# Two activation rows loaded once and spread by the array, and the first weight group moved to another DMA queue

## The chip, the cores and the metric

The kernel runs on one core of a Trainium2 chip. The metric is device time in microseconds; executions of a program can fall into a fast and a slower state, and all runs below were in the fast one, except e4, a single look without a state. Every ratio is to runs of the kernel before on the same chip. A ratio is the mean time of one kernel's runs over that of the other's of the same rounds, so it is not quite the ratio of the medians that are quoted.

## The reference, cut to what matters

One token goes through a layer norm, an attention with 32 heads over a cache of 8192 keys and values, and a gated MLP; the kernel returns the output and all gradients, including those of the two caches.

```python
# x, grad_out: (1, 1, 640)   k_cache, v_cache: (1, 32, 8192, 128)   all bf16
# wq: (640, 4096)  wo: (4096, 640)  w1, w3: (640, 1728)  w2: (1728, 640)
def _fwd_reference(...):
    xn = _layernorm(x, axis=-1)
    return x + _A_ref(xn, k_cache, v_cache, wq, wo) + _B_ref(xn, w1, w3, w2)

def reference(...):
    out, vjp = jax.vjp(f, x, k_cache, v_cache, wq, wo, w1, w3, w2)
    return (out, *vjp(grad_out))
```

Each head reads 2 MB of K and 2 MB of V and writes 2 MB of dK and 2 MB of dV. That is most of the 304 MB that the kernel moves.

## The kernel before

The SP queue is a first-in, first-out list of K and V loads, dK and dV stores and the MLP's weights. The weights wq and wo come in eight groups of four heads. Group 0 stands on the SP queue just behind K of head 0; all later groups are on the GpSimd queue. x and grad_out are loaded as broadcasts, one copy per partition, on the ACT queue.

```python
nc.scalar.dma_start(x_bc_bf, A_x.rearrange("a b d -> (a b d)").partition_broadcast(P))
nc.scalar.dma_start(g_bc[:], grad_out.rearrange("a b d -> (a b d)").partition_broadcast(P))

def load_group(g, eng):
    wq_g = wpool.tile([P, NC, GW], BF16, name="wq_g", tag="wq_g")
    eng.dma_start(wq_g[:], wq_v[:, :, g * GW:(g + 1) * GW])      # rows of 1024 B
    wo_g = wpool.tile([P, GH, D], BF16, name="wo_g", tag="wo_g")
    eng.dma_start(wo_g[:], wo_v[:, g * GH:(g + 1) * GH, :])      # rows of 1280 B
    grp[g] = dict(wq=wq_g, wo=wo_g)

lag = [1]
def load_next():                       # next K or V load, if enough of the ten slots are free
    if not pending or len(free_slots) < lag[0]:
        return
    kind, h = pending.pop(0)
    t = free_slots.pop(0)
    fifo(t[:], (kc if kind == "K" else vc)[h])        # fifo = nc.sync.dma_start
    kv_tiles[(kind, h)] = t

load_next()                            # K of head 0
load_group(0, nc.sync)
for _ in range(3):
    load_next()                        # V 0, K 1, V 1; then the MLP's weights, K 2, V 2
# ... cut ...
lag[0] = 3
```

What head 0 needs before it can multiply with the keys is prepared here. prep_q needs wq and the normalised x; prep_do needs wo and g_bc; the later steps need both.

```python
def prep_do(g, hh):
    # four dot products over wo, one per head, on VectorE
    nc.vector.scalar_tensor_tensor(junk[:], G_["wo"][:, hh, :], 1.0, g_bc[:], ALU.mult, ALU.mult,
                                   accum_out=G_["do"][:, hh:hh + 1])
# ... cut ...
T(0, "K", 0); T(0, "K", 1)
prep_q(0, ps_0[:, 0:GH], True)         # 20 small matmuls over wq
for hh in range(GH):
    prep_do(0, hh)
prep_sel(0, ...); prep_cm(0, ...); fill_qz(0); rows_pe(0, ...); rows_act(0)
for h in range(H):
    if h == MLP_AT:                    # MLP_AT = 2
        outers_a(h - 1); outers_b(h - 1)
        mlp()
    head(h)                            # stores dV and dK of head h - 1 on the SP queue, each after its outer product
```

## Time and profile before

| | before |
|---|---|
| time, median of 3 runs | 734.95 us (734.04 to 735.1) |
| bytes moved, mean rate over the span | 303.9 MB, 414 GB/s |
| wo of group 0 landed | 14.40 us |
| first maximum of head 0 | 28.55 us |
| first store issued (dV of head 0) | 44.27 us |
| dV of head 2 issued | 124.79 us |

In the profile's lines PE is the array's matmul and PEld its weight load, DVE is VectorE, ACT ScalarE, POOL GpSimd and SP SyncE; a q after the name marks an instruction of that engine's queue that issues a DMA transfer; L108 is a line of the kernel. "kv" is any of the ten slots.

Two parts of the page of the kernel before: what was moved in each of 40 equal slices, and the DMA queues with their packets, MB and share of 16 engines' span. q1 is the SP queue, q0 GpSimd's, q10 ACT's.

```profile
GB/s 337 401 410 420 425 428 423 400 421 422 417 422 426 429 427 424 427 430 426 429 425 428 429 420 427 429 429 427 425 428 427 428 432 428 428 431 429 422 390 154
...
q1 hardware_dynamic: 21328, 276.39, 89.3%
q0 software_dynamic: 5728, 26.30, 8.9%
...
q10 hardware_dynamic: 308, 0.33, 0.1%
```

The DMA is the limit. The two big queues fill 98% of the engines' time, and the rate is between 400 and 432 GB/s from the second slice to the 38th. Only the first slice and the last two are clearly lower. Time can be lost only where the queues run dry or where packets are slow.

The start, from the timeline of the kernel before (start, duration, engine, line, operation, out<-in; in brackets the idle time before it and what ended it):

```profile
1.19 0.42 SPq L108 DMA_DIRECT2D wq_g<-in_A_wq_dram  x1
1.66 0.52 SPq L110 DMA_DIRECT2D wo_g<-in_A_wo_dram  x1
...
9.96 0.10 PEld L221 LDWEIGHTS <-x_kt 1*128 1x128 bf16 x1 [9.96 <-DMA x_kt<-in_A_x_dram]
...
13.11 0.62 PEld L249 LDWEIGHTS <-wq_g 128*128 128x128 bf16 x20 [0.64 <-DMA wq_g<-in_A_wq_dram]
...
14.51 0.83 DVE L240 SCALAR_TENSOR_TENSOR side<-wo_g,g_bc 128x640 bf16<-128x640 bf16 x1 [1.05 <-DMA wo_g<-in_A_wo_dram]
...
18.75 0.17 DVE L336 COPY qz<-cm_g 128x8 bf16<-128x8 bf16 x1
```

The x broadcast lands at 9.96, wq at 13.1, and wo last: VectorE starts its dot products at 14.51, and at 18.75 the query is in place for head 0. In the pieces of the chain of waits up to 80 us there is one transfer only, this one of wo, with 12.75 us. Everything after it up to the MLP is compute. The first maxima of heads 0 and 1 come at:

```profile
28.55 0.23 DVE L355 TENSOR_REDUCE mrow<-m 128x1 f32<-128x64 f32 x1 [9.62 <-PE m L329]
47.31 0.23 DVE L355 TENSOR_REDUCE mrow<-m 128x1 f32<-128x64 f32 x1 [0.87 <-PE m L329]
```

The SP queue before its first store of head 2, from the same timeline, and the four-microsecond stretches around it (us; busy time of PE, PEld, DVE, ACT and POOL; then the array's granted clock, the busy share of the DMA engines, GB/s):

```profile
111.78 0.33 SPq L102 DMA_DIRECT2D kv<-in_A_v_cache_dram  x1
124.79 0.34 SPq L102 DMA_DIRECT2D out_dram<-kv  x1
128.07 0.33 SPq L102 DMA_DIRECT2D kv<-in_A_k_cache_dram  x1
```

```profile
120.00:124.00 4.00, 4.00 (x47) 2.36 (x44) 3.96 (x4) 2.28 (x6) 0.00 (x0) 1.00 0.97 405
124.00:128.00 4.00, 4.00 (x38) 3.07 (x35) 3.85 (x5) 2.99 (x7) 0.00 (x0) 1.00 1.01 420
128.00:132.00 4.00, 3.48 (x47) 2.60 (x46) 3.23 (x10) 2.43 (x7) 0.00 (x0) 1.00 0.99 388
```

Between 111.78 and 124.79 nothing is issued on SP. What had been issued by then lasted just long enough: the share stays at 1. So there is next to no reserve at this point (counted from the issues and the packet records, 0.2 MB of the SP queue's bytes are still under way at 124.7 us), and the store waits for compute (dV of head 2 follows its outer product on VectorE).

How the later groups fare on the GpSimd queue, from the issues of the kernel before (count, KB, median us from issue to landing):

```profile
wq_g<-in_A_wq_dram POOLq DMA_DIRECT2D x7, 640.0 KB, 13.2
wo_g<-in_A_wo_dram POOLq DMA_DIRECT2D x7, 640.0 KB, 19.5
```

### The profile page before, as it was taken

Reading aid. Unit: us, or ns where it says so; the run is one execution under the profiler, and the core shown is the slowest. Engines: PE = TensorE matmul, PEld = TensorE weight load, DVE = VectorE, ACT = ScalarE, POOL = GpSimd, SP = SyncE. Lnnn points to the kernel's source line nnn. Section 1 sums busy time; section 2 is a strip of 40 time slices with the busy share of each in tenths; the row PEclk is TensorE's granted clock in tenths of the full one; section 3 lists DMA queues with packets and bytes.
Section 4 is the critical chain, followed back from the end, with each engine's and each line's share of the span. In section 5 each row is a group of like instructions: output and inputs, shape, how many; then the busy total and the mean of one; then the engine's idle time right before and its main releaser. Section 6 shows DMA issues by size and latency. Waiting matters only on the chain.

```text
span 733.2 us, 13850 instructions
## 1 busy us (share of the span) xinstructions
PE 608.6 (83%) x5663; PEld 425.9 (58%) x5663; DVE 461.1 (63%) x806; ACT 367.9 (50%) x716; POOL 30.0 (4%) x45
## 2 busy tenths in 40 slices
PE   1998579998899889988999797888698888899840
PEld 1666457666666666665666565555475566666520
DVE  4059655677766666667767755646746576477482
ACT  1650726665465455655565554545464455554510
POOL 0010010000100000000000000000000000000000
PEclk9996699999899889988899988989989799888965
DMA  9999999999999999999999999999999999999993
GB/s 337 401 410 420 425 428 423 400 421 422 417 422 426 429 427 424 427 430 426 429 425 428 429 420 427 429 429 427 425 428 427 428 432 428 428 431 429 422 390 154
DMA packets 27428, 303.90 MB, mean 414 GB/s; under 512 B 2836, under 2 KB 4436, under 8 KB 10724
## 3 DMA queue, kind: packets, MB, share of 16 engines
q1 hardware_dynamic: 21328, 276.39, 89.3%
q0 software_dynamic: 5728, 26.30, 8.9%
q8 instruction: 44, 0.72, 0.4%
q10 hardware_dynamic: 308, 0.33, 0.1%
q14 instruction: 20, 0.16, 0.1%
HBM read 151.67 MB, written 151.34 MB: 413 GB/s over the span
## 4 chain that ended last, share of the span: by engine, by line
PE 42%; DMA 41%; ACT 7%; DVE 7%; issue 2%; SPq 0%; ACTq 0%; DVEq 0%
PE pT L294 19%; DMA kv<-in_A_k_cache_dram 18%; DMA out_dram<-kv 17%; PE m L329 6%; PE X L406 5%; ACT KT L296 4%; DMA kv<-in_A_v_cache_dram 4%; PE sA L313 3%; PE dA L313 2%; DVE kv L439 2%; DMA wo_g<-in_A_wo_dram 2%; ACT kv L589 1%; PE gu_ps L516 1%; DVE side L240 1%; ACT KT L319 1%
## 5 line engine op out<-in xcount | busy, mean ns | idle before, releaser
L296 ACT COPY KT<-pT 128x512 f32<-128x512 f32 x512 | 290.4, 590 | 235.7 <-PE pT L294 204.3
L294 PE MATMUL pT<-ident_f,kv 128*128 128x128 f32 x2048 | 321.8, 298 | 36.5 <-DMA kv<-in_A_k_cache_dram 27.3
L294 PEld LDWEIGHTS pT<-ident_f,kv 128*128 128x128 f32 x2048 | 251.7, 156 | 93.2 <-PE pT L294 29.5
L439 DVE TENSOR_TENSOR kv<-qd,U 128x4096 bf16<-128x4096 bf16 x64 | 146.1, 2285 | 0.0
L439 DVE TENSOR_TENSOR kv<-qd,P 128x4096 bf16<-128x4096 bf16 x64 | 143.6, 2285 | 0.0
L329 PEld LDWEIGHTS m<-selc,KT 128*128 128x128 f32 x512 | 67.6, 206 | 47.1 <-ACT KT L319 37.4
L329 PE MATMUL m<-selc,KT 128*128 128x16 f32 x512 | 73.7, 277 | 24.4 <-ACT KT L319 24.2
L406 PE MATMUL X<-kv,Z 128*32 128x512 bf16 x1024 | 84.9, 460 | 1.8 <-DVE Z L423 1.8
L389 DVE SCALAR_TENSOR_TENSOR U<-m,P 128x64 bf16<-128x64 f32 x32 | 7.4, 233 | 105.4 <-PE m L329 105.4
L313 PE MATMUL sA<-KT,qz 128*32 128x512 bf16 x512 | 55.4, 423 | 0.0
L313 PE MATMUL dA<-KT,qz 128*32 128x512 bf16 x512 | 54.5, 412 | 0.2 <-ACT KT L296 0.2
L313 PEld LDWEIGHTS <-qz 128*32 128x32 bf16 x1024 | 26.5, 93 | 42.7 <-issue 41.6
L406 PEld LDWEIGHTS <-Z 128*32 128x32 bf16 x1024 | 28.7, 110 | 34.0 <-issue 17.0
L355 DVE TENSOR_REDUCE mrow<-m 128x1 f32<-128x64 f32 x32 | 7.2, 224 | 60.9 <-PE m L329 60.9
L349 ACT CAST qd<-pT 128x256 bf16<-128x256 f32 x32 | 11.9, 373 | 49.3 <-DVE kv L439 31.6
L489 DVE SCALAR_TENSOR_TENSOR wq_g<-wq_g,side 128x512 bf16<-128x512 bf16 x40 | 27.3, 683 | 0.0
L240 DVE SCALAR_TENSOR_TENSOR side<-wo_g,g_bc 128x640 bf16<-128x640 bf16 x32 | 26.2, 820 | 1.4 <-DMA wo_g<-in_A_wo_dram 1.0
L362 DVE TENSOR_REDUCE negM<-m 128x1 f32<-128x128 f32 x32 | 9.3, 292 | 25.2 <-PE m L359 25.2
L421 DVE SCALAR_TENSOR_TENSOR U<-m,P 128x128 bf16<-128x128 f32 x32 | 11.4, 355 | 19.3 <-PE m L419 19.3
L379 DVE RECIPROCAL rZ<-m 128x1 f32<-128x1 f32 x32 | 5.3, 167 | 24.2 <-PE m L373 24.2
L319 ACT COPY KT<-dA 128x512 f32<-128x512 f32 x32 | 19.4, 605 | 0.6 <-PE dA L313 0.6
L319 ACT COPY KT<-sA 128x512 f32<-128x512 f32 x32 | 19.3, 602 | 0.0
(143 smaller groups left out, 363.2 us busy)
## 6 DMA issues: line engine op xcount, KB each, us to landing
out_dram<-kv SPq DMA_DIRECT2D x64, 2048.0 KB, 31.0
kv<-in_A_k_cache_dram SPq DMA_DIRECT2D x32, 2048.0 KB, 25.1
kv<-in_A_v_cache_dram SPq DMA_DIRECT2D x32, 2048.0 KB, 26.3
out_dram<-wo_g POOLq DMA_DIRECT2D x8, 640.0 KB, 12.0
out_dram<-wq_g POOLq DMA_DIRECT2D x8, 640.0 KB, 13.0
wq_g<-in_A_wq_dram POOLq DMA_DIRECT2D x7, 640.0 KB, 13.2
wo_g<-in_A_wo_dram POOLq DMA_DIRECT2D x7, 640.0 KB, 19.5
kv<-in_B_w_dram SPq DMA_DIRECT2D x2, 1728.0 KB, 27.1
```

Source lines behind the costliest of these rows:

```text
L240: nc.vector.scalar_tensor_tensor(junk[:], G_["wo"][:, hh, :], 1.0, g_bc[:], ALU.mult, ALU.mult, accum_out=G_["do"][:, hh:hh + 1])
L294: nc.tensor.transpose(pT[:, k * P:(k + 1) * P], W3[:, 4 * c + k, :], ident_f[:])
L296: nc.scalar.copy(KT[:].rearrange("p k w -> p (k w)"), pT[:])
L313: nc.tensor.matmul(S_[kind][q:q + QW, :], lhsT=S_["qz"][:, o:o + QW], rhs=KTb[:, par, :], start=(c0 == 0), stop=(c0 == NCH - 2), skip_grou ...
L319: nc.scalar.copy(XS[:].rearrange("p k w -> p (k w)"), S_.pop(kind)[:])
L329: nc.tensor.matmul(S_["m"][:, b0:b0 + J].rearrange("p (c k t) -> p k c t", k=4, t=2)[:, k, :, :], lhsT=XS[:, k, :], rhs=selc[:].rearrange( ...
L349: nc.scalar.copy(qd[:].rearrange("p a d -> p (a d)"), hd[h].pop("ps_r"))
L362: nc.vector.tensor_reduce(S_["negM"][:], S_["m"][:, 2 * J:2 * J + P], AX.X, ALU.max, negate=True)
L406: nc.tensor.matmul(xg["X"][q:q + QW, :], lhsT=Z[:, o:o + QW], rhs=W[:, N4 * i:N4 * (i + 1)], start=(slot == 0 and i < 4), stop=(slot == NS ...
L421: nc.vector.scalar_tensor_tensor(S_["U2"][:], S_["V"][:, 0:J].unsqueeze(2).to_broadcast([P, J, 2]), S_["m"][:, OC + NS:OC + NS + 1], S_["P ...
L439: nc.vector.tensor_tensor(dst[:, lo * DH:hi * DH].rearrange("p (j a b) -> p j a b", a=DH // 2, b=2), vec.rearrange("p (a b) -> p a b", b=2 ...
L489: nc.vector.scalar_tensor_tensor(wq_g[:, ci, :], wq_g[:, ci, :], 1.0, dqb, ALU.mult, ALU.mult, accum_out=dxa[:, ci, g:g + 1])
```

## The change

The intent was to drop 0.33 MB of broadcasts, to get x early, and to let the first weight group run beside K of head 0 in place of standing behind it. The diff in full:

```diff
--- before.py
+++ after.py
@@ -92,11 +92,14 @@
     NSLOT = 10
     RW = 64
 
-    x_kt = tpool.tile([P, 4, P], F32, name="x_kt", tag="KT")
-    x_bc_bf = x_kt[:].rearrange("p k w -> p (k w)").bitcast(BF16)[:, 0:D]
-    nc.scalar.dma_start(x_bc_bf, A_x.rearrange("a b d -> (a b d)").partition_broadcast(P))
+    rows_in = []
+    for src in (A_x, grad_out):
+        r_kt = tpool.tile([P, 4, P], F32, name="row_kt", tag="KT")
+        row = r_kt[0:1].rearrange("p k w -> p (k w)").bitcast(BF16)[:, 0:D]
+        nc.scalar.dma_start(row, src.rearrange("a b d -> (a b) d"))
+        rows_in.append(row)
+    x_row, g_row = rows_in
     g_bc = consts.tile([P, D], BF16, name="g_bc")
-    nc.scalar.dma_start(g_bc[:], grad_out.rearrange("a b d -> (a b d)").partition_broadcast(P))
 
     def fifo(out_, in_):
         nc.sync.dma_start(out_, in_)
@@ -125,7 +128,7 @@
         kv_tiles[(kind, h)] = t
 
     load_next()
-    load_group(0, nc.sync)
+    load_group(0, nc.gpsimd)
     for _ in range(3):
         load_next()
     mC = free_slots.pop(0)
@@ -209,22 +212,30 @@
         return ps_t.tile([P, 512], F32, name="pT", tag="pT")
 
     ln3 = consts.tile([P, 3], F32, name="ln3")
-    msum, sumsq, std = ln3[:, 0:1], ln3[:, 1:2], ln3[:, 2:3]
-    nc.vector.tensor_reduce(msum, x_bc_bf, AX.X, ALU.add)
-    nc.vector.tensor_scalar(negmean[:], msum, -1.0 / D, None, ALU.mult)
-    nc.vector.scalar_tensor_tensor(t_tile()[:, 0:D], x_bc_bf, negmean[:], x_bc_bf, ALU.add, ALU.mult,
-                                   accum_out=sumsq)
-    nc.scalar.activation(std, sumsq, ACTF.Sqrt, bias=eps_t[:], scale=1.0 / D)
-    nc.vector.reciprocal(rstd[:], std)
+    xsum, sumsq, std = ln3[:, 0:1], ln3[:, 1:2], ln3[:, 2:3]
     ps_xg = pst()
+    ps_g = pst()
     for ci in range(NC):
-        nc.tensor.matmul(ps_xg[:, ci:ci + 1], lhsT=x_bc_bf[0:1, ci * P:(ci + 1) * P], rhs=one_bf[0:1, :],
+        nc.tensor.matmul(ps_xg[:, ci:ci + 1], lhsT=x_row[:, ci * P:(ci + 1) * P], rhs=one_bf[0:1, :],
                          start=True, stop=True)
-        nc.tensor.matmul(ps_xg[:, NC + ci:NC + ci + 1], lhsT=g_bc[0:1, ci * P:(ci + 1) * P], rhs=one_bf[0:1, :],
+        nc.tensor.matmul(ps_xg[:, NC + ci:NC + ci + 1], lhsT=g_row[:, ci * P:(ci + 1) * P], rhs=one_bf[0:1, :],
                          start=True, stop=True)
+    nc.tensor.matmul(ps_xg[:, P:P + D - 512], lhsT=one_bf[0:1, :].to_broadcast([1, P]), rhs=g_row[:, 512:D],
+                     start=True, stop=True)
+    nc.tensor.matmul(ps_g[:], lhsT=one_bf[0:1, :].to_broadcast([1, P]), rhs=g_row[:, 0:512],
+                     start=True, stop=True)
+    nc.scalar.copy(g_bc[:, 0:512], ps_g[:])
+    nc.scalar.copy(g_bc[:, 512:D], ps_xg[:, P:P + D - 512])
     nc.vector.tensor_copy(x_col[:], ps_xg[:, 0:NC])
     nc.vector.tensor_copy(g_col[:], ps_xg[:, NC:2 * NC])
-    nc.vector.tensor_scalar(xn_col[:], x_col[:], negmean[:], rstd, ALU.add, ALU.mult)
+    nc.vector.tensor_reduce(xsum, x_col[:], AX.X, ALU.add)
+    nc.tensor.matmul(ps_xg[:, 16:17], lhsT=ones_b, rhs=xsum, start=True, stop=True)
+    nc.vector.tensor_scalar(negmean[:], ps_xg[:, 16:17], -1.0 / D, None, ALU.mult)
+    nc.vector.scalar_tensor_tensor(xn_col[:], x_col[:], negmean[:], x_col[:], ALU.add, ALU.mult, accum_out=sumsq)
+    nc.tensor.matmul(ps_xg[:, 17:18], lhsT=ones_b, rhs=sumsq, start=True, stop=True)
+    nc.scalar.activation(std, ps_xg[:, 17:18], ACTF.Sqrt, bias=eps_t[:], scale=1.0 / D)
+    nc.vector.reciprocal(rstd[:], std)
+    nc.vector.tensor_scalar(xn_col[:], x_col[:], negmean[:], rstd[:], ALU.add, ALU.mult)
     nc.vector.tensor_copy(xn_col_bf[:], xn_col[:])
 
     def prep_new(g):
@@ -791,7 +802,7 @@
     nc.vector.tensor_scalar(nst[:], ps_f[:, 0:2], -1.0 / D, None, ALU.mult)
     t5 = consts.tile([P, NC], F32, name="t5")
     nc.vector.scalar_tensor_tensor(t5[:], xn_col[:], nst[:, 1:2], dxn[:], ALU.mult, ALU.add)
-    nc.vector.tensor_scalar(t5[:], t5[:], nst[:, 0:1], rstd, ALU.add, ALU.mult)
+    nc.vector.tensor_scalar(t5[:], t5[:], nst[:, 0:1], rstd[:], ALU.add, ALU.mult)
     nc.vector.tensor_tensor(fin[:, NC:2 * NC], t5[:], g_col[:], ALU.add)
     ps_o = pst()
     nc.tensor.transpose(ps_o[0:2 * NC, 0:P], fin[:], ident_f[:])
```

## The prediction

> What bounds the kernel. The transfers: the table of queues gives the SP queue 89.3% and the GpSimd queue 8.9% of the 16 engines' time. 303.9 MB move at 414 GB/s mean, 428 in later slices, 337 in the first. Time is bytes over rate, plus start, tail, and any stretch in which the queues run dry.
>
> The start hangs on compute. The chain of waits up to 78 us is: transfer of the first wo group (12.75 us, lands 14.40), four dot products on VectorE (0.86 us each), head 0, head 1, the MLP; no KV load is in it. Issued minus finished bytes, the backlog is used up near 125 us, when head 2's V store is issued (124.79, after waiting for VectorE). Afterwards the backlog grows to 5 MB by 300 us: transfers set the pace and a lost microsecond is not regained. So a delay of head 0 comes through nearly in full.
>
> What the change does.
> 1. The two broadcasts (0.33 MB, rows of 1280 B) become two rows. By the packet records they held the engines about 1.2 us: saved. x lands at 3 to 4 us in place of 9.94.
> 2. Norm statistics and the spread of grad_out move to the array: some ten steps of 0.15 to 0.6 us, 3 to 4 us against 3 before, done before the weights land. Neutral.
> 3. wq and wo of group 0 leave the SP queue, where they stood just behind K of head 0, for the GpSimd queue. On SP they moved in 1024 and 1280 B packets[...]; on GpSimd packets are 4096 and 5120 B (160 to 200 ns): about 0.8 us saved. But later groups show what that queue costs beside a full SP queue: 4.2 us from issue to first packet, then one small packet for each 16 KB packet of SP. That engines take turns between queues packet by packet is also what the Trainium skill says ("DMA: Bandwidth & Descriptors", Queues, rings and completion order); the trace agrees (equal packet counts of both queues while a group loads). Issue to landing is 13.2 us for wq and 19.5 us (17.6 to 21.0) for wo, issued 0.9 us later. Issued at 0.7 us, wo lands at about 21, not 14.4.
>
> Sum: head 0 starts 5 to 7 us later; head 2's store moves to about 131; the DMA idles there, and the 2 us of transfer saved only widen the hole. Net about +5 us.
>
> Predicted: 740 us, 8 in 10 between 735 and 744.5. Faster by over 2%: 0.01; within: 0.96; slower: 0.03.
>
> Right if: wo of group 0 lands at 19 to 22 us and the first dot product starts there; the first maximum of head 0 (28.55) moves to 33 to 36; the first store (44.27) to 49 to 51; head 2's V store to 129 to 132, with DMA share clearly below 1 just before it; x lands before 5 us; GB/s from 2 to 10 us rises. Wrong if: wo lands before 15 us, head 0 has caught up by 125 us, or the DMA stays full there.
>
> What would make it wrong. The GpSimd queue may start quicker at an empty start, or get larger turns; then only the saving of 1 to 2 us is left (733). The granted clock is half from 57.7 to 71.4 and from 78 to 92 us; another phase may give or take some us of the MLP.

## More of the kernel before

The experiments ran on several chips, where the median of the kernel before was between 733.68 and 734.95 us, so two versions of different rounds are compared by their ratios.

The MLP uses four of the ten slots for its weights and gives them back when its gradients are stored.

## The result and the profile after

| | before | after |
|---|---|---|
| time, median of 6 runs each | 734.83 us | 740.35 us (738.44 to 742.38) |
| ratio, with 95% interval | | 1.0075 (1.0054 to 1.0095) |
| span of the profiled run | 733.2 us | 738.7 us |

The 0.75% is clear of noise.

The start of the kernel after, from its timeline:

```profile
1.29 0.99 POOL L111 DMA_DIRECT2D wq_g<-in_A_wq_dram  x1 [0.84 <-POOLq L828]
1.30 0.23 ACTq L99 DMA_DIRECT2D row_kt<-in_grad_out_dram  x1
2.05 0.10 PEld L219 LDWEIGHTS <-row_kt 1*128 1x128 bf16 x1 [2.05 <-DMA row_kt<-in_A_x_dram]
2.28 0.77 POOL L113 DMA_DIRECT2D wo_g<-in_A_wo_dram  x1
...
6.57 0.10 PEld L221 LDWEIGHTS <-row_kt 1*128 1x128 bf16 x1 [4.41 <-DMA row_kt<-in_grad_out_dram]
...
11.37 0.17 DVE L239 CAST xn_col_bf<-xn_col 128x5 bf16<-128x5 f32 x1
...
15.19 0.61 PEld L260 LDWEIGHTS <-wq_g 128*128 128x128 bf16 x20 [3.27 <-DMA wq_g<-in_A_wq_dram]
...
21.85 0.83 DVE L251 SCALAR_TENSOR_TENSOR side<-wo_g,g_bc 128x640 bf16<-128x640 bf16 x1 [9.85 <-DMA wo_g<-in_A_wo_dram]
...
26.10 0.17 DVE L347 COPY qz<-cm_g 128x8 bf16<-128x8 bf16 x1
```

x is there at 2.05 and the normalised x at 11.5 (line L239). wq lands at 15.2, and wo at 21.85 in place of 14.40. The dot products are the same four; qz is filled at 26.10 in place of 18.75, which is 7.35 us later. The first maxima of heads 0 and 1:

```profile
36.54 0.23 DVE L366 TENSOR_REDUCE mrow<-m 128x1 f32<-128x64 f32 x1 [10.27 <-PE m L340]
53.89 0.23 DVE L366 TENSOR_REDUCE mrow<-m 128x1 f32<-128x64 f32 x1 [0.93 <-PE m L340]
```

They are 8.0 and 6.6 us later than before. The 1.4 us between go with the granted clock (see "Why the prediction was right").

The SP queue and the stretches around dV of head 2, after:

```profile
116.91 0.33 SPq L105 DMA_DIRECT2D kv<-in_A_v_cache_dram  x1
131.12 0.34 SPq L105 DMA_DIRECT2D out_dram<-kv  x1
```

```profile
120.00:124.00 4.00, 3.95 (x44) 2.45 (x44) 1.47 (x6) 3.44 (x9) 0.00 (x0) 1.00 1.07 453
124.00:128.00 4.00, 3.93 (x45) 2.66 (x42) 2.09 (x5) 1.34 (x3) 0.00 (x0) 1.00 0.47 195
128.00:132.00 4.00, 4.00 (x38) 2.79 (x37) 4.00 (x3) 2.95 (x6) 0.00 (x0) 1.00 0.07 29
132.00:136.00 4.00, 4.00 (x36) 3.18 (x36) 3.21 (x7) 2.98 (x7) 0.00 (x0) 1.00 1.07 430
```

The store is issued 6.3 us later, and from 124 to 132 us the DMA has little to do: the two shares, 0.47 and 0.07, leave 4 * 0.53 + 4 * 0.93 = 5.8 us idle. VectorE and the array are at work (2.09 and 4.00, and 3.93 and 4.00 us of each four); they are on their way to the store that would feed the DMA.

The page of the kernel after, the same parts:

```profile
GB/s 354 402 418 387 418 432 345 344 412 424 417 410 426 430 427 420 429 431 426 424 426 429 428 428 423 425 432 426 427 427 426 429 429 429 428 429 428 428 400 163
...
q10 hardware_dynamic: 24, 0.01, 0.0%
```

Slices of about 18.5 us: the first is faster (354 against 337), the seventh and eighth are the hole (345 and 344 against 423 and 400), and later ones are alike. The fourth is lower too (387 against 420): from 64 to 72 us the rate is 336 GB/s against 421, a smaller dent where the SP queue waited for the delayed stores of head 1. The engines' busy share was still 0.97 there: from 66 to 70 us they worked almost alone on the GpSimd queue's records of 4096 and 5120 B. 8 us * 85 GB/s are 0.68 MB, or 1.6 us.

**A ledger of bytes.** Summing the packet records up to 152 us gives 61.41 MB before and 58.80 MB after. The totals are 303.95 and 303.63 MB. So 242.54 MB were left before and 244.83 after, 2.29 MB more. Both kernels move 426 to 427 GB/s from 152 to 690 us, so that is 2.29 / 0.427 = 5.4 us. The spans differ by 5.5 us. The whole loss is made before 152 us.

### The profile page after: what moved, and what is told of

It is laid out like the page before. It is cut to its first block, busy times and chain, and to the rows that moved or that the text cites. A ratio compares the mean times of both kernels' runs of the same rounds, so it can differ in the third digit from the quotient of the medians.

```text
span 738.7 us, 13870 instructions
## 1 busy us (share of the span) xinstructions
PE 606.3 (82%) x5669; PEld 424.8 (58%) x5669; DVE 459.3 (62%) x806; ACT 368.3 (50%) x719; POOL 31.5 (4%) x47
## 4 chain that ended last, share of the span: by engine, by line
PE 50%; DMA 29%; ACT 9%; DVE 8%; issue 2%; ACTq 0%; POOL 0%; DVEq 0%; SPq 0%; POOLq 0%
PE pT L305 23%; DMA kv<-in_A_k_cache_dram 15%; DMA out_dram<-kv 8%; PE m L340 7%; ACT KT L307 5%; PE X L417 5%; PE sA L324 5%; DMA kv<-in_A_v_cache_dram 4%; PE dA L324 3%; DVE kv L450 3%; DMA wo_g<-in_A_wo_dram 3%; ACT KT L330 2%; DVE side L251 1%; ACT kv L600 1%; PE gu_ps L527 1%
## 5 line engine op out<-in xcount | busy, mean ns | idle before, releaser
L417 PE MATMUL X<-kv,Z 128*32 128x512 bf16 x1024 | 82.9, 451 | 1.8 <-DVE Z L434 1.8
L417 PEld LDWEIGHTS <-Z 128*32 128x32 bf16 x1024 | 28.6, 109 | 32.9 <-issue 15.2
L251 DVE SCALAR_TENSOR_TENSOR side<-wo_g,g_bc 128x640 bf16<-128x640 bf16 x32 | 26.2, 820 | 10.2 <-DMA wo_g<-in_A_wo_dram 9.8
L432 DVE SCALAR_TENSOR_TENSOR U<-m,P 128x128 bf16<-128x128 f32 x32 | 11.4, 355 | 18.9 <-PE m L430 18.9
```

Of the source, the lines that this page charges most:

```text
L417: nc.tensor.matmul(xg["X"][q:q + QW, :], lhsT=Z[:, o:o + QW], rhs=W[:, N4 * i:N4 * (i + 1)], start=(slot == 0 and i < 4), stop=(slot == NS ...
L432: nc.vector.scalar_tensor_tensor(S_["U2"][:], S_["V"][:, 0:J].unsqueeze(2).to_broadcast([P, J, 2]), S_["m"][:, OC + NS:OC + NS + 1], S_["P ...
```

## The experiments

Theory: wo of group 0 comes late on the GpSimd queue because the engines take turns between queues, one packet each, and its packets are small beside SP's; head 0 starts late; the lateness reaches dV of head 2, where the DMA has no reserve, and becomes idle DMA time. Rivals: the rows and the norm on the array cost the time; the GpSimd queue is slow by its own descriptor work; the late start costs through compute and the idle DMA is only a mark of it.

The landings in the text below are the starts of the first dot product or of the q matmuls that waited for them; the issue times are from the timelines.

### Rows without the queue, and the queue without the rows

```diff
 # e1_rows_only, on the kernel after
-    load_group(0, nc.gpsimd)
+    load_group(0, nc.sync)
 # e2_queue_only, on the kernel before
-    load_group(0, nc.sync)
+    load_group(0, nc.gpsimd)
```

> The changed kernel with group 0 back on the SP queue (rows and column-sum statistics kept). Theory (the queue of group 0 is the whole loss): wo of group 0 lands at 12 to 13.5 us, head 2's V store is issued at 122 to 124, the DMA has no hole near 126 us, and the saved broadcasts show as 1 to 2 us: 733 us. Rival (the rows, the longer norm chain or the spreading of grad_out cost the time): 738 to 740 us.

Measured: 733.02 us, ratio to before 0.9992 (0.9978 to 1.0005). wo landed at 13.36, dV of head 2 was issued at 121.52, and no stretch of 4 us from 40 to 180 us moved less than 390 GB/s.

> The kernel before with group 0 alone moved to the GpSimd queue (broadcasts kept). Theory: wo lands at 20 to 22 us, head 2's V store at 130 to 132, a DMA hole of about 5 us before it, 740 to 742 us. Rival (rows and norm part): 734 to 735 us as before.

Measured: 741.94 us, ratio 1.0109 (1.0095 to 1.0123). wo landed at 23.66, dV of head 2 was issued at 132.59, and there is the hole (DMA shares 0.79, 0.06 and 0.72):

```profile
124.00:128.00 4.00, 3.93 (x46) 2.61 (x44) 0.70 (x5) 2.15 (x4) 0.00 (x0) 1.00 0.79 332
128.00:132.00 4.00, 4.00 (x46) 2.41 (x46) 4.00 (x3) 2.36 (x5) 0.00 (x0) 1.00 0.06 25
132.00:136.00 4.00, 4.00 (x35) 3.19 (x36) 3.64 (x5) 3.00 (x6) 0.00 (x0) 1.00 0.72 303
```

The queue move alone makes the loss and more; the rows are not its cause. They save a little: e1 against before does not resolve it from zero, e5 and e9 below do.

### The same queue, the other order

```diff
 # e3_wo_first, on the kernel after; group 0 only
-        wq first, then wo
+        wo first, then wq
```

> The changed kernel with wo of group 0 issued before wq on the GpSimd queue: same queue, same bytes, only the order turned. Theory (the time at which head 0 can start goes through one to one): wo lands at about 13 us, wq at about 22; the short q part (0.9 us) then replaces the dot products (3.5 us) behind the last landing, head 0 and head 2's V store come 2.5 to 3 us earlier than in the changed kernel (store at about 128.3), time about 737.5 us. Rival (the GpSimd queue itself slows the start, whoever waits for it): 740 us unchanged.

Measured: 737.55 us (735.66 to 738.84), ratio 1.0049 (1.0029 to 1.0069). wo landed at 13.36, wq at 21.38; dV of head 2 was issued at 128.52. Same queue, same bytes: 2.6 us earlier at that store, and by the ratios (1.0049 against 1.0075) 1.9 us less time, give or take 2.1. The two intervals overlap, so the time alone does not settle it; the store does. It speaks for the time at which head 0 has all it needs, and against a tax of the queue as such; e7 below shows that more clearly.

### Why the landing is late: turns

```diff
 # e4_act_queue, on the kernel after
-    load_group(0, nc.gpsimd)
+    load_group(0, nc.scalar)
 # e7_small_sp_packets, on the kernel after: K 0, V 0 and K 1 in four column quarters each
-        fifo(t[:], (kc if kind == "K" else vc)[h])
+        parts = 4 if h < 2 and (kind, h) != ("V", 1) else 1
+        for r in range(parts):
+            w = KVN // parts
+            fifo(t[:, r * w:(r + 1) * w], (kc if kind == "K" else vc)[h][:, r * w:(r + 1) * w])
```

> The changed kernel with group 0 on the ACT queue, a hardware queue. Theory (engines take turns between queues packet by packet, and this queue's packets are 1024 and 1280 B, 72 per engine): each small packet waits for a 16 KB packet of SP (0.65 us), wo lands only at about 45 to 52 us, head 2's V store near 160, about 768 us. Rival (the cost of the GpSimd queue is its software descriptor work[...]): wo lands at 10 to 14 us, 733 to 735 us.

Measured: 748.11 us in one run. The waits for the two weights in its timeline:

```profile
28.53 0.61 PEld L260 LDWEIGHTS <-wq_g 128*128 128x128 bf16 x20 [16.29 <-DMA wq_g<-in_A_wq_dram]
32.59 0.83 DVE L251 SCALAR_TENSOR_TENSOR side<-wo_g,g_bc 128x640 bf16<-128x640 bf16 x1 [20.27 <-DMA wo_g<-in_A_wo_dram]
```

A hardware queue was slower than GpSimd's, by 10.7 us at the landing of wo. The packet records, in stretches of 2 us, show the turns (q1 is SP, q10 ACT):

```
us from the span's start    SP packets, mean bytes    ACT packets, mean bytes
 9.6 to 11.6                49, 16384                 49, 1024
11.6 to 13.6                62, 12685                 62, 1024
13.6 to 15.6                51, 15742                 50, 1024
15.6 to 17.6                47, 16384                 47, 1024
```

One for one, within one packet. The expected 45 to 52 us and 768 us were missed, because I took SP's packets to stay at 16 KB; from about 24 us on the MLP's weights were sent, whose packets are smaller (mean 5060 B, then 1497 B for a while), so the turns became short, and 520 KB of group 0 went in 2 us. In part of that time SP had hardly anything to send: from 30 to 31 us there are 61 records of SP and 239 of ACT. As e4 is one run, its landings count here more than its time.

> The changed kernel, group 0 on the GpSimd queue, with the first three SP loads (K and V of head 0, K of head 1) each issued in four column quarters, so that their packets are 4096 B and not 16384 B. Theory (one packet of each queue in turn): GpSimd's packets now wait 0.16 us and not 0.65, both queues get about half, wo lands at 12 to 15 us in place of 21.8, head 0 starts about as in the kernel before, 733 to 735 us. Rival (the GpSimd queue is slow by itself, by its descriptor work): wo lands at 20 to 22 us, 740 us.

Measured: 734.24 us, ratio 0.9997 (0.9983 to 1.001). Its waits for the two weights:

```profile
10.66 0.61 PEld L263 LDWEIGHTS <-wq_g 128*128 128x128 bf16 x20 [0.92 <-DMA wq_g<-in_A_wq_dram]
13.72 0.83 DVE L254 SCALAR_TENSOR_TENSOR side<-wo_g,g_bc 128x640 bf16<-128x640 bf16 x1 [3.89 <-DMA wo_g<-in_A_wo_dram]
```

Group 0 was still on the GpSimd queue, in the same 288 records of 4096 and 5120 B. Only SP's packets were smaller, and wo landed 8.1 us earlier; the whole loss was gone. Most of that is shorter turns: from the first to the last record of group 0 it took 7.9 us (5.34 to 13.23) in place of 15.4 (6.00 to 21.36), and the first record came 0.7 us earlier. Both runs speak for turns and against a slowness of the GpSimd queue by itself.

### Does an earlier start give anything?

```diff
 # e5_group_before_k, on the kernel after; e9_before_group_first: the same two lines on the kernel before
-    load_next()
-    load_group(0, nc.gpsimd)          (nc.sync in the kernel before)
+    load_group(0, nc.sync)
+    load_next()
```

> The changed kernel with group 0 on the SP queue ahead of K of head 0. Theory (hinge: a later head 0 costs one to one, but once the DMA has no hole near 125 us an earlier one gives nothing): wo lands at 6 to 8 us, q waits for the norm chain (about 11.5), head 0 starts 2 us earlier than with group 0 behind K, head 2's V store at 118 to 121, no hole, and the time is that of the version with group 0 behind K on SP, 732 to 734 us. Rival (each microsecond at the start counts): 730 to 731 us.

Measured: 732.4 us, ratio 0.9971 (0.9959 to 0.9984): the fastest version, 2.1 us under before and clear of noise. The dot products began at 9.84 and q at 14.18, since its matmuls stand on the array behind the first transposes of K, and K, now sent second, landed at 12.45. dV of head 2 was issued at 121.81, a little later than e1's, contrary to the expected 118 to 121; no hole.

> The kernel before, broadcasts and all, with group 0 issued on the SP queue ahead of K of head 0: the order alone, without the rows. Theory (before has no DMA hole to begin with, so an earlier head 0 gives nothing, and only bytes and packet time saved count): 733.5 to 735 us, the same as before, although head 0 starts 1 to 3 us earlier. Rival (each microsecond at the start counts): 731.5 to 733 us.

Measured: 734.14 us, ratio 1.0000 (0.9988 to 1.0012). Head 0's first maximum came at 28.5, no earlier than before, so the expected earlier head 0 did not come about (q at 16.72, behind transposes that waited for K until 14.99); dV of head 2 was issued at 122.85, 1.9 us earlier than before, and the time stayed. 1.5 of the 1.9 us are not the order's doing: head 1's first maximum follows head 0's by 17.3 us in place of 18.8, in a stretch where the granted clock of this profiled execution was not halved.

So a later store costs, and one that came 1.9 us earlier was worth nothing within 0.9 us. That an earlier start of head 0 gives nothing was not tested as planned: e9's head 0 was not earlier, and the 1.4 us by which e5's first maximum led e1's (25.47 against 26.86) were used up in the MLP's stretch (64.5 us against 62.9), so that their stores came at the same time. e5 and e9 differ only by the rows: 0.9971 against 1.0000, about 2 us for them, give or take 1.3. (e1 against before gave 0.6, with an interval from a saving of 1.6 us to a loss of 0.4.)

### Filling the hole

```diff
 # e6_extra_load, on the kernel after, at the end of mlp()
         free_slots.append(mC)
         load_next()
+        lag[0] = 1
+        load_next()
+        lag[0] = 3
 # e8_lead_kept: instead of these three lines
+        lag[0] = 2
+        load_next()
 #            and before head 8
+        if h == 8:
+            lag[0] = 3
```

> The changed kernel, group 0 still on the GpSimd queue, with one KV load (K of head 6, into a slot that the MLP has given back) let go before head 2's V store instead of after it. The start of the chain is untouched. Theory (the loss is the DMA's idle time before that store): head 0 and the V store stay late (36 and 131 us), but the hole (about 6 us) is mostly filled, and 3 to 5 of the 6 us come back: 735.5 to 737 us. Rival (the late start costs through compute all along, the hole is only a mark of it): 740 us.

Measured: 738.9 us (738.07 to 739.76), ratio 1.0057 (1.0041 to 1.0072), a miss: 1.4 us under the changed kernel's 740.35, not 3 to 5, and not clear of noise, since the interval overlaps that of the changed kernel (1.0054 to 1.0095). Its stretches:

```profile
124.00:128.00 4.00, 3.93 (x44) 2.73 (x42) 0.72 (x6) 2.18 (x5) 0.00 (x0) 1.00 0.70 296
128.00:132.00 4.00, 4.00 (x46) 2.36 (x44) 3.96 (x4) 2.27 (x6) 0.00 (x0) 1.00 0.82 285
...
136.00:140.00 4.00, 3.48 (x47) 2.59 (x45) 3.27 (x10) 2.40 (x7) 0.00 (x0) 1.00 0.83 352
140.00:144.00 4.00, 3.15 (x41) 1.93 (x37) 1.79 (x3) 2.43 (x5) 0.00 (x0) 1.00 0.50 205
```

The first hole is smaller, but a second one stands at 136 to 144. The load was only borrowed: with three free slots needed, the store of dV gave no new load, and before the next store the DMA lacked those 2 MB. Idle time from the two holes is 4 * (0.30 + 0.18 + 0.17 + 0.50) = 4.6 us against 5.8, 1.2 us less. Taken alone, e6 decides nothing.

> The changed kernel, group 0 on the GpSimd queue, with one KV load more in flight from the end of the MLP to head 8 (two free slots are enough to let a load go, not three), so that the load let go early is not taken back at the next store, as it was in the run with a single extra load, where the idle time only moved from 126 to 140 us. Theory (the loss is DMA idle time, and work put into it comes back): the start stays late (head 2's V store at about 131), idle time from 124 to 145 us falls from about 6 to 1 to 3 us, 735 to 737.5 us. Rival (the late start costs through compute, idle DMA is only a mark): 739 to 741 us.

Measured: 737.38 us (734.79 to 739.53), ratio 1.0039 (1.0022 to 1.0056). The start stayed late (wo at 21.91, dV of head 2 at 132.04). The shares from 124 to 140 us were 0.57, 0.49, 1.09 and 0.91: some 4.1 us idle, more than the expected 1 to 3, because the extra load went out only at 129.28: the waits of the SP queue from 117 to 130 us are all for stores to land. The trace is of an execution of 739.07 us, one of the slower of the six. By the ratios (1.0039 against 1.0075) 2.6 us of the loss came back, give or take 1.9, with head 0 as late as ever. That is against the rival by which compute carries the whole loss.

> The fastest version so far (rows kept, group 0 on SP ahead of K) with the one more load in flight from the MLP to head 8. Theory (there is no hole left to fill): no gain, 732 to 733 us, ratio to before 0.996 to 0.999. Rival (the DMA still waits a little for the stores between 125 and 160 us): 730 to 731.5 us.

Measured: 734.03 us, ratio 0.9998 (0.9986 to 1.001), slower than e5. The SP queue around dV of head 2:

```profile
107.53 0.33 SPq L105 DMA_DIRECT2D kv<-in_A_v_cache_dram  x1
124.83 0.33 SPq L105 DMA_DIRECT2D kv<-in_A_k_cache_dram  x1
125.25 0.40 SPq L105 DMA_DIRECT2D out_dram<-kv  x1
```

Here the extra load made a hole of its own. It waited until 124.83 for a slot whose store was under way, and dV of head 2 stood behind it until 125.25, although its outer products (the two halves, 4.49 us from 114.92) had ended at 119.4. The share from 124 to 128 us was 0.74. On a first-in, first-out queue, a load that waits for a slot holds up a store that is ready.

### All runs in one ledger

Bytes moved by 152 us are summed from the packet records; "by the ledger" is the difference to before of what was then left to move, divided by 427 GB/s; the spans are those of the profiled runs.

| run | wo of group 0 usable, us | dV of head 2 issued, us | MB moved by 152 us (of total) | by the ledger, us | span less before's, us |
|---|---|---|---|---|---|
| before | 14.51 | 124.79 | 61.41 (303.95) | 0 | 0 |
| after | 21.85 | 131.12 | 58.80 (303.63) | +5.4 | +5.5 |
| e1 rows only | 13.36 | 121.52 | 62.27 (303.63) | -2.8 | -2.2 |
| e2 queue only | 23.66 | 132.59 | 58.42 (303.95) | +7.0 | +7.1 |
| e3 wo first | 13.36, wq 21.38 | 128.52 | 59.78 (303.63) | +3.1 | +2.0 |
| e4 ACT queue | 32.59 | 140.15 | 54.94 (303.62) | +14.4 | +13.1 |
| e5 group before K | 9.84, q 14.18 | 121.81 | 62.18 (303.63) | -2.6 | -2.7 |
| e6 extra load | 22.16 | 132.76 | 58.78 (303.63) | +5.4 | +4.8 |
| e7 small SP packets | 13.72 | 122.70 | 61.81 (303.63) | -1.7 | -1.3 |
| e8 lead kept | 21.91 | 132.04 | 59.28 (303.63) | +4.2 | +4.1 |
| e9 before, group first | 10.78, q 16.72 | 122.85 | 61.82 (303.95) | -1.0 | -1.5 |
| e10 e5 and lead kept | 9.96, q 14.27 | 125.25 | 61.10 (303.63) | 0.0 | -1.3 |

(In e4 the DMA also ran dry from 52 to 60 us, with shares of 0.04 and 0.46.) Within 1.3 us, what a version has moved by 152 us fixes the span of its profiled execution. These are single executions, and those of e1 to e4 are from a chip on which the kernel before was about 1.2 us faster than in the first row's rounds. By the ratios, e1 is at -0.6 us, e2 at +8.0, e3 at +3.6, e7 at -0.2, e8 at +2.9 and e9 at 0.0, so the ledger and the mean times agree within 2.2 us only. That is the hinge: where the store comes later than the DMA's work lasts, the bytes fall behind and never catch up; where it comes earlier, they are nearly the same (at most 0.9 MB, or 2 us, ahead).

## Why the prediction was right

It said 740 us (735 to 744.5), and 740.35 was measured. Point by point:

- **The limit and where it has no reserve: right.** The DMA was full to the point where dV of head 2 was issued, and idle just before it when that store came late. The Trainium skill's rule of turns ("DMA: Bandwidth & Descriptors", section "Queues, rings and completion order") agrees with the traces; e4 shows it at 49 packets to 49, e7 from the other side. The prediction's 5 MB of backlog at 300 us does not come out of the trace: issues less landed bytes of the SP queue are 10 MB there.
- **Landing of wo at 19 to 22 us: right, 21.85.** The issue-to-landing time was 19.6 us, as for the later groups (19.5); the issue was at 2.28, about 0.7 us later than I assumed.
- **First maximum of head 0 at 33 to 36: 36.54, just outside; first store at 49 to 51: 50.78; dV of head 2 at 129 to 132: 131.12; share below 1 before it: 0.47 and 0.07.** From qz to the first maximum it took 10.4 us, against 9.8 before: the array's first eight-transpose steps took 1.7 to 2.0 us until 32.8, and 1.1 after that; before, the shorter steps began at 23.7. x landed before 5 us: 2.05. The rate from 2 to 10 us rose from 309 to 371 GB/s.
- **"3 to 4 us" for the norm on the array: mis-sized.** It took from 3.98 to 11.54, 7.6 us. (x was there at 2.05, but the column of ones that it is multiplied with came only at 3.9, behind steps of GpSimd that now stood after its issues of group 0.) The matmuls for x and grad_out alternate, and grad_out's row landed only at 6.57; then x_col waited until 8.35 for ScalarE's two copies of the spread grad_out. (The activation table load of 1.28 us behind these copies ended at 9.61, before its function's input was there at 10.5.) It cost nothing, as wq came at 15.2.
- **"2 us of transfer saved": a little less.** By 24 us, 0.36 MB more had been moved than before, and 0.33 MB no longer had to be: 0.69 MB, 1.6 us at 427 GB/s. The part for group 0's larger packets, 0.8 us in the prediction, was 0.3: its records held the 16 engines for 3.75 us on SP before and for 3.44 on GpSimd after.
- **Missed: the dent at 64 to 72 us.** It and the hole together are 5.8 + 1.6 = 7.4 us; less the 1.6 us saved this is 5.8, against 5.5 measured. It did not change the sum: bytes not moved at 64 us were moved before 124, and without the dent the hole would have begun that much earlier.
- **The granted clock: some luck.** Head 0's first maximum was 8.0 us late, dV of head 2 only 6.3. From the first maximum of head 0 to that of head 1 it took 18.8 us before, with 3.4 us at half the clock in it, and 17.35 after, with none. In e1, e3, e4, e5, e6, e7, e8 and e10 the half-clock piece stands there and the stretch is 18.5 to 18.9 us; in e2 and e9 it is missing as after, and the stretch is 17.2 and 17.3. In e8, with wo usable at nearly the same time (21.91), the store came at 132.04. So without this piece of luck the store would have been at about 132.5, outside the 129 to 132 of the prediction, and the time, as an estimate from these numbers, 1 to 1.5 us longer, still inside its range. Where that piece falls in executions that were not profiled is not known.
- **The MLP stretch**, from head 1's first maximum to head 2's, was 64.6 us before and 64.3 after, so it did not decide. Over all versions it lay between 62.9 (e1, e4, e10) and 64.8 (e6). In the four with 62.9 to 63.3 (e7 too) the last half-clock piece of 3.4 us begins 3.4 us after the long one before it, in the others 10.2 us after; that this is the reason was not tested.

## What to carry to other kernels

Where a kernel is limited by transfers, look for the moment at which the queues hold no reserve, and follow the chain of compute back from the store that refills them: here a store that came 4 to 15 us late cost nearly all of that, and one that came 1.9 us early gained nothing that could be measured. In these traces a small transfer on a queue of its own was not ahead of a bulk stream but in turns with it, one packet each, so its small packets waited beside large ones; if it is needed first, put it first on the same queue, or cut the bulk stream's packets at the start. Before letting loads run further ahead on a first-in, first-out queue, ask whether they will make a ready store wait.

## What the Trainium skill lacked or had wrong

- "DMA: Bandwidth & Descriptors", section "Issuing engines are not separate DMA queues", says that starting DMAs from several engines only saves the time to initiate them. Here the queue decided when the same 1.31 MB landed: wo was usable at 13.36 us behind K on SP (e1), at 21.85 on GpSimd, at 32.59 on ACT (e4).
- The same page, section "Queues, rings and completion order", gives about 9 to 17 descriptors as a typical packet that is drained in one turn. For the SP and ACT queues the records here show turns of one record each: one of 1024 B for one of 16384 B (49 to 49 in 2 us of e4); whether a record is one descriptor the trace does not say. GpSimd's records were of 4096 and 5120 B for the same rows of 1024 and 1280 B, so the same transfer took fewer turns there. The page's turns hold; what it lacks is what the size ratio does to the smaller stream.
- The same page, table "Specifications", gives about 0.6 us (hardware) and 1 us (software) to the first byte. With idle engines the row of x came 0.9 us after its issue (0.74 to 1.65). Beside a just started stream of 16 KB packets, the row of grad_out (1280 B on ACT, issued at 1.30) began only at 5.53, 4.2 us later, and group 0 on GpSimd (issued at 1.29) only at 6.00. With 4 KB packets on SP (e7) grad_out began at 3.84, but GpSimd still only at 5.34. No page read has this wait for the first turn; why it is so long was not tested.
